# A new written-out order for a linear-attention and MLP kernel on one core, and shorter rows for the loads of r and v

## The chip, the cores and the metric

The kernel runs on one core of one Trainium2 chip. The metric is the device time of one execution in microseconds, the median of several runs. Engines are called as in the profile: PE is TensorE's matmuls and PEld its weight loads, DVE is VectorE, ACT is ScalarE, POOL is GpSimd, SP is SyncE. DMAs are issued by SP or by POOL.

## The reference

Four batches of eight heads run a recurrence over 768 steps with a state of 40x40 per head; its output, 3072 tokens of 320, goes through an MLP with softplus inside erf.

```
for t in range(768):
    y[:, :, t] = einsum('bhd,bhde->bhe', r_t, state)
    Sa = einsum('bhde,bhe->bhd', state, a_t)
    state = state * w_t[:, :, None, :] - einsum('bhd,bhe->bhde', Sa, b_t) \
          + einsum('bhd,bhe->bhde', v_t, k_t)
x = y.transpose(0, 2, 1, 3).reshape(3072, 320)
h = x @ w_in                      # 320 x 2048
out = (h * erf(softplus(h))) @ w_out   # 2048 x 320
```

## The kernel before

The recurrence is done in chunks of 32 steps. Two groups of 16 heads each run 24 chunks; four chunks (128 steps) make a stage, so there are 12 stages and 48 chunks. For each stage `prep` loads the decays w and makes their running products with two scans on VectorE (lines 631 and 635). For each chunk `aphase` loads k, b and a as one tile bk, scales it (lines 666 and 671), multiplies (A, line 676), masks (line 683), and sends a part to DRAM (AD). Once per stage `tphase` reads it back as Ti, solves a triangular system on VectorE by 28 short instructions (lines 723 and 724), sends the result out (TD) and back (Tb), transposes it (R, line 732) and finishes it with two groups of small matmuls (W and DAD, both line 739) and two VectorE steps (743, 746).

`chain` is what depends on the state, chunk after chunk: Z (line 784), a copy zt, U (line 793), a copy us into the tile Us, four transfers Vu<-Us, the transpose UT (line 820) of Us into pQ, the copy vtu into the tile vt, PQ (line 829) from vt, its mask on VectorE into Vu (line 832), MY (lines 840 and 844), and the update of the state MT (line 847) and of the output (Ym, line 851). vt is loaded for each chunk by one DMA called rv (line 770): r in two blocks of 32 columns, v in one, and the last 32 columns are filled by vtu. Every copy has line 570 on ScalarE or 572 elsewhere, every DMA line 575.

When a stage's outputs have gone through DRAM (xw, xr), the MLP takes its 256 tokens in eight tiles of 256 hidden columns: mm1 (line 1005, two blocks a tile), a copy hc, tanh, two logs, exp, two VectorE steps (1038, 1039), gelu, two more steps (1050, 1051), and mm2 (line 1060, four blocks a tile). Four tiles make a unit, which shares three loads of ScalarE's tables.

The MLP's weights come as 64-bit floats, and are taken apart at the start by VectorE, ScalarE and GpSimd (lines 931 to 962): from chunks of w_in in the tile wo, and of w_out in the tiles h.

All operations are first recorded by `Plan.add`, with what they read and write and which engines may do them. `Plan.schedule` could order them by its own rules, but when the tables ORDER and ENGINES fit, it takes them as they stand: ORDER is the order in which the operations are issued (each engine's instructions stand in its own queue in that order), ENGINES says who does each one, and an entry of −1 in ORDER is a filler, a matmul of constants into a bank that is not in use (`warm`, line 578). TensorE executes its queue in order, fillers too.

Of the kernel before, what the change touches and what calls it, by code (L numbers as in the profile page):

```python
# [1193 lines left out]
```

## Time and profile before

| what | value |
|---|---|
| median of 3 runs | 866.4 us (865.0 to 875.59) |
| the profiled execution, its own time | 870.61 us |
| its span, first to last instruction | 868.8 us |
| mean granted clock of TensorE | 0.959 |
| instructions | 32556, of them 13793 matmuls |
| DMA | 107.63 MB in 120213 packets |

Busy time is counted per engine; matmuls are pipelined, so a busy PE is not PE at its peak. "Idle before" is the time for which an engine stood still ahead of an instruction, with the last thing it waited for; "issue" is time in which nothing that the profile shows held it. The chain that ended last is followed back from the last instruction. A row of a timeline has its start, its length, the engine, the line and operation, out<-in, and in brackets the idle time before it.

### The profile page before, as it was taken

The numbers are of one execution on the slowest core, as the hardware profiler recorded it, in microseconds if no ns is written. First come the engines' busy times: TensorE is split into PE (matmuls) and PEld (weight loads), VectorE is DVE, ScalarE is ACT, GpSimd is POOL, SyncE is SP. The second block draws the span as 40 slices with busy tenths as digits, with TensorE's granted clock in tenths as the row PEclk, the third lists the DMA queues.
The fourth block names the chain that finished last, engine by engine and source line by source line (L and its number), as shares of the span: only waits on it lengthen the run. The fifth ranks groups of instructions, "written<-read, shape, count | busy, mean of one in ns | idle before, by whom it ended". The sixth has DMA issues, their size and how long they took to land.

```text
span 868.8 us, 32556 instructions
## 1 busy us (share of the span) xinstructions
PE 748.4 (86%) x13793; PEld 581.5 (67%) x13793; DVE 649.9 (75%) x1372; ACT 562.2 (65%) x1052; POOL 347.8 (40%) x493
## 2 busy tenths in 40 slices
...
PEclk9998999999999999998999899999998999998998
...
GB/s 238 200 182 171 181 155 147 116 144 125 143 118 138 144 151 107 133 135 113 159 119 122 119 141 130 145 99 165 119 144 101 102 117 96 71 62 53 19 15 19
DMA packets 120213, 107.63 MB, mean 124 GB/s; under 512 B 76397, under 2 KB 99285, under 8 KB 120061
## 3 DMA queue, kind: packets, MB, share of 16 engines
...
q8 instruction: 110, 1.80, 0.9%
...
## 4 chain that ended last, share of the span: by engine, by line
PE 40%; DMA 22%; DVE 16%; issue 10%; ACT 7%; POOL 3%; SPq 1%; DVEq 0%; POOLq 0%; ACTq 0%
PE po L1060 12%; PE ph L1005 10%; DMA Vu<-Us 5%; DMA Tb<-TD 3%; PE my L840 3%; DMA TD<-Ti 2%; DMA Zs<-Ab 2%; PE ph L578 2%; PE pA L739 2%; DMA AD<-Zs 2%; DVE nd L1038 2%; DVE h L1051 2%; PE pA L676 2%; PE pQ L811 2%; DMA Ti<-AD 2%
## 5 line engine op out<-in xcount | busy, mean ns | idle before, releaser
L1060 PE MATMUL po<-wo,h 128*128 128x320 f32 x768 | 254.6, 462 | 9.0 <-DVE h L1051 9.0
L1060 PEld LDWEIGHTS po<-wo,h 128*128 128x128 f32 x768 | 139.9, 199 | 54.3 <-DVE h L1051 10.1
L1013 ACT ACTIVATE l<-l 128x512 f32<-128x512 f32 x192 | 111.2, 625 | 15.8 <-DVE nd L1038 14.5
L1005 PE MATMUL ph<-xh,wih 128*128 128x256 f32 x384 | 99.9, 342 | 2.2 <-ACT h L570 1.2
L575 POOL DMA_DIRECT2D Vu<-Us x93 | 52.7, 570 | 113.7 <-ACT Us L570 73.4
L1005 PE MATMUL ph<-xl,wih 128*128 128x256 f32 x384 | 78.9, 287 | 2.1 <-issue 2.1
L1005 PE MATMUL ph<-xh,wil 128*128 128x256 f32 x384 | 78.2, 286 | 0.0
L840 PE MATMUL my<-Vu,sg 64*40 64x72 f32 x1536 | 53.5, 240 | 27.5 <-DMA Vu<-Us 16.6
L1051 DVE SCALAR_TENSOR_TENSOR h<-l,h 128x512 f32<-128x512 f32 x96 | 71.8, 757 | 5.1 <-POOL l L1050 4.3
L1039 DVE SCALAR_TENSOR_TENSOR r<-nd,r 128x512 f32<-128x512 f32 x96 | 70.7, 737 | 4.1 <-POOL nd L1038 3.0
L1005 PEld LDWEIGHTS ph<-xh,wih 128*128 128x128 f32 x384 | 63.8, 196 | 13.3 <-issue 1.9
L840 PEld LDWEIGHTS my<-Vu,sg 64*40 64x40 f32 x1536 | 40.9, 120 | 42.2 <-issue 11.9
L1013 ACT ACTIVATE l<-h 128x512 f32<-128x512 f32 x96 | 56.7, 627 | 12.0 <-DVE h L1051 8.3
L1038 DVE TENSOR_TENSOR nd<-l,r 128x512 f32<-128x512 f32 x79 | 55.1, 698 | 11.5 <-ACT r L1013 9.2
L578 PE MATMUL ph<-d 104*128 104x512 bf16 x256 | 63.6, 395 | 0.0
L1050 DVE TENSOR_TENSOR l<-l,r 128x512 f32<-128x512 f32 x77 | 58.3, 760 | 4.4 <-ACT l L1013 3.9
L1005 PEld LDWEIGHTS ph<-xl,wih 128*128 128x128 f32 x384 | 61.4, 196 | 0.0
L1005 PEld LDWEIGHTS ph<-xh,wil 128*128 128x128 f32 x384 | 60.9, 195 | 0.0
L570 ACT COPY Zm<-MT 40x320 f32<-40x320 f32 x63 | 28.7, 456 | 48.0 <-DVE MT L847 39.8
L570 ACT COPY h<-ph 128x512 f32<-128x512 f32 x79 | 45.7, 583 | 18.8 <-PE ph L1005 13.8
L676 PE MATMUL pA<-Ab,bk 104*64 104x64 f32 x720 | 32.6, 230 | 27.6 <-DVE bk L671 20.7
L1013 ACT ACTIVATE r<-r 128x512 f32<-128x512 f32 x96 | 55.2, 624 | 0.4
...
## 6 DMA issues: line engine op xcount, KB each, us to landing
bk<-in_kba_e POOLq DMA_DIRECT2D x26, 416.0 KB, 4.7
vt<-in_rv_e POOLq DMA_DIRECT2D x25, 416.0 KB, 4.5
vt<-in_rv_e SPq DMA_DIRECT2D x23, 416.0 KB
bk<-in_kba_e SPq DMA_DIRECT2D x19, 416.0 KB
...
```

Source lines behind the costliest of these rows:

```text
L570: self.nc.scalar.copy(o, i)
L575: self.P.add(name, "SP", lambda e: self.eng(e).dma_start(o(), i()), rd, wr, pr, ISSUE.get(name, 0.41))
L578: self.nc.tensor.matmul((self.ph[1], self.pQ)[x], self.d1[:, :128], self.d1[:, :512], start=True, stop=True)
L676: nc.tensor.matmul(pa[i % 2 * 64:i % 2 * 64 + 64, i // 4, i // 2 % 2], bk[:, i].rearrange("p a b -> p (a b)"), ab[:, :, i], start=True, st ...
L840: nc.tensor.matmul(my[h * 64:h * 64 + 40, x, j], sg[xs, j, h], vu[xs, j // 2 * 2 + h, j % 2], start=True, stop=False)
L1005: nc.tensor.matmul(ph[:, j * 256:j * 256 + 256], a[:k, fs], b[:k], start=(m == 0), stop=(m == 7))
L1013: self.P.add(name, "ACT", lambda e: nc.scalar.activation(out=o, in_=i, **kw), rd, wr + ["act"], pr, 0.62)
L1038: P.add("nd", [("DVE", 0.69), ("POOL", 1.28)], lambda e, r=r, l=l, nd=nd: s.eng(e).tensor_tensor(out=nd, in0=l, in1=r, op=ALU.mult), [("l" ...
L1039: P.add("rho", "DVE", lambda e, r=r, nd=nd: nc.vector.scalar_tensor_tensor(out=r, in0=nd, scalar=2 * C4, in1=r, op0=ALU.add, op1=ALU.mult) ...
L1050: P.add("E", [("POOL", 1.28), ("DVE", 0.69)], lambda e: s.eng(e).tensor_tensor(out=l, in0=l, in1=r, op=ALU.mult), [("r", ir)], [("l", il)] ...
L1051: P.add("G", "DVE", lambda e: nc.vector.scalar_tensor_tensor(out=h, in0=l, scalar=-1.0, in1=h, op0=ALU.add, op1=ALU.mult), [("l", il)], [( ...
L1060: nc.tensor.matmul(po, h[:, bs], s.wo[:, f], start=(f == 0), stop=(f == 15))
```

## The change

Four things change.

- ORDER and ENGINES are other tables of the same form. The count of fillers goes from 256 to 216. Of the operations that may be done by two engines, some change hands: VectorE has 1303 operations of the list (1332 before), ScalarE 1063 (1038), GpSimd 499 (489), SP 493 (500).
- rv has 80 rows instead of 104 and loads 96 of 128 columns. Before, the two heads of a pair began at rows 0 and 64 with 24 rows of zeros between; now they stand at 0 and 40, and the product over rows has 80 of them.
- Us is stored without gaps (four times 40 columns), is no longer zeroed at the start, and its transpose has 80 rows.
- A unit of the MLP is given as a list of sizes, [4] * 24, which gives the same units. The scratch size for DMA descriptors is written out with the value 16384, which is the default.

```diff
 ORDER = (
-    3, 7, 9, 20, 4, 6, 10, 18, 348, 144, 12, 22, 147, 11, 21, 145, 146, 16, 149, 23, 126, 129, 24, 148, 352, 135, 138, 351, 14, 17, 41, 53, 0, 15, 13,
+    7, 11, 143, 15, 16, 146, 19, 3, 6, 9, 8, 4, 17, 5, 144, 12, 22, 351, 23, 145, 21, 125, 128, 147, 148, 24, 126, 25, 0, 28, 134, 127, 152, 153, 27,
...
+SCRATCH = 16384
...
-    rv = np.zeros((NG, 24, 104, NP, 4, 32), np.float32)
-    rv[..., :2, :] = diag(el(r)).transpose(0, 1, 2, 4, 3, 5)
-    rv[..., 2, :] = stk(el(v))
-    o["rv_e"] = np.ascontiguousarray(rv[:, :, :, [pair(n) for n in range(NP)]]).reshape(NG, 24, 104, NP * 128)
+    rv = np.zeros((NG, 24, 2, 40, NP, 3, 32), np.float32)
+    for h in range(2):
+        rv[:, :, h, :, :, h] = el(r)[:, :, h]
+    rv[..., 2, :] = el(v)
+    o["rv_e"] = np.ascontiguousarray(rv[:, :, :, :, [pair(n) for n in range(NP)]]).reshape(NG, 24, 80, NP * 96)
...
-        s.US = ring("Us", K["us"], [128, NQ // 2, 128])
+        s.US = ring("Us", K["us"], [128, NQ, 40])
...
-        for n, R in (("zs", s.ZS), ("zm", s.ZM), ("us", s.US)):
+        for n, R in (("zs", s.ZS), ("zm", s.ZM)):
...
-        vr = s.VT[ivt]
+        vr = s.VT[ivt][:80]
...
-        s.dma("rv", lambda: vr, lambda: I["rv_e"][g, ck].rearrange("p (a x) -> p a x", a=NP), wr=[("vt", ivt, 0), ("vt", ivt, 1)], pr=prl)
+        s.dma("rv", lambda: vr[:, :, :96], lambda: I["rv_e"][g, ck].rearrange("p (a x) -> p a x", a=NP), wr=[("vt", ivt, 0), ("vt", ivt, 1)], pr=prl)
...
-                nc.tensor.transpose(put[:, y], us[:, y, 0:104], s.ident)
+                nc.tensor.transpose(put[:, y], us[:, 2 * y:2 * y + 2].rearrange("p h e -> p (h e)"), s.ident)
```

Line numbers after the change are one higher up to line 1020. Two places show what the tables move. First VectorE's queue in the solve of stage 0 (lines 723 and 724; 724 and 725 now), where an instruction that takes apart a chunk of w_out in the tile h (line 931, now 932) stands between the steps. Before:

```order
L723 TENSOR_TENSOR tmp_106<-Ti 128x50
L724 TENSOR_TENSOR Ti<-Ti,tmp_106 128x5x10
L931 TENSOR_SCALAR r_140<-h 128x512
L723 TENSOR_TENSOR tmp_106<-Ti 128x54
L724 TENSOR_TENSOR Ti<-Ti,tmp_106 128x6x9
```

Now:

```order
L724 TENSOR_TENSOR tmp_106<-Ti 128x56
L725 TENSOR_TENSOR Ti<-Ti,tmp_106 128x8x7
L932 TENSOR_SCALAR r_140<-h 128x512
L724 TENSOR_TENSOR tmp_106<-Ti 128x54
L725 TENSOR_TENSOR Ti<-Ti,tmp_106 128x9x6
```

It moved from behind the fifth step of the solve to behind the eighth. Second TensorE's queue at the first chunk of stage 3, around PQ (line 829, now 830) and the start of MY (lines 840 and 844, now 841 and 845); line 1060 is a block of mm2, lines 676 and 694 are the next stage's A and the transpose of its bk. Before:

```order
L1060 MATMUL po_161<-wo,h 128x320
L829 MATMUL pQ<-vt_107 64x2x32 x8
L676 MATMUL pA<-Ab_76,bk_100 64x2x32 x8
L840 MATMUL my<-Vu_78,sg_95 40x72 x4
L844 MATMUL my<-Rt_81,Sm_80 40x32 x4
```

Now:

```order
L677 MATMUL pA<-Ab_76,bk_100 64x2x32 x8
L830 MATMUL pQ<-vt_107 64x2x32 x8
L1060 MATMUL po_161<-wo,h 128x320
L695 MATMUL pA<-ident,bk_100 128x104 x4
L1060 MATMUL po_160<-wo,h 128x320
L841 MATMUL my<-Vu_78,sg_95 40x72 x4
L845 MATMUL my<-Rt_81,Sm_80 40x32 x4
```

The A block moved ahead of PQ, and two mm2 blocks and the transpose moved between PQ and MY.

More of the change, by code (lines that the diff above doesn't have):

```diff
@@ new lines @@
+    "AAAVGVVAAAVSAVVAVSVSSVPVVGGPAGGSGVPVVGSPVGGSGVPVVSSPAGVSSVPVVGSPAGGGGGVAPAPAAVAAPAPVPVPVVGSGGGAAPAPAAAAAPAPAPVPVVSSSGGAAPAPAAAAAPAPAPVPVVGGS"
+    "SSVAPAPAAVVAPVPAPVPVVSSSGGGGGAAVVVVVVVVVVVVVVVVVVVVVVVVVVVVGGGGVPPPPVPPPPVGAVGAVGGAGPPAAPPAAPPAAPPAAAAAAAAAAAAAAAAVVVVVVVVAAAAAPPVAPPAAVVPPP"
+    "PPPAAGVPPPPPPAAVVPPPPVVPPPPSAVVAVSVSGVPVVSGPASVGSVPVVSGPASVGSVPVVSGPAGVSSVPVVGSPASGGSSVVVPAPAGSSSPAPAPVPVVGGGGSAAPVPAGSSSPAPAPVPVVSGGGGVVPVP"
+    "ASSGGPVPAPVPVVGGGSGAAPAPAGGGSPAPAPVPVVSSGSGGGSAAVVVVVVVVVVVVVVVVVVVVVVVVVVVVSGSSVPPPPVPPPPVSAGSAGSGVVAAAAAAAAAAAAAAVVVVVVVVAAAAAPPVAPPAAGVPP"
@@ new lines @@
+    "PPPPAAGVPPPPPPAAVVPPPPVVPPPPASASAAAAAAAAAAAAAAVVGVVVVVAAAAAPPAAPPAAVVPPPPPPAAGVPPPPPPAAVVPPPPVVPPPPSAVVVVGGGGGPVVSGPVSGSGVPVVSGPVGGGGVPVVGGP"
+    "AGVSSVPVVSSPAGGSGGGAAPAPASGSSPVPVPVPVVSSSSSAAPAPASGSGPAPAPVPVVSSSGSAVPAPAGGGGPAPAPVPVVGSGGSAAPAPVGGSGPAPAPVPVVGSGSSGGSAAVVVVVVVVVVVVVVVVVVVV"
+    "VVVVVVVVGSSGVPPPPVPPPPVGVVSAVGSVVAAAAAAAAAAAAAAVVVVGVVVAAAAAPPAAPPAAVVPPPPPPAAVVPPPPPPAAVVPPPPVVPPPPASASAAAAAAAAAAAAAAVVVVGVGVAAAAAPPAAPPAAV"
+    "VPPPPPPAAVVPPPPPPVAGVPPPPVVPPPPSAVVVVGVSGVPVVGSPAGVSSVPVVGSPVGVSSGPVVSGPAGVGGGPVVGSPAGGSSSVAAPVPAGSGSPAPAPVPVVSSGSSAVPVPASGGSPVPAPVPVVSSGSGA"
@@ new lines @@
+    "APAPAGGSSPAPAPVPVVSSGGGAAPAPAGGSGPAPAPVPVVSSSGSGGSAAVVVVVVVVVVVVVVVVVVVVVVVVVVVVSSGSVPPPPVPPPPVSVGSAGSSVGAAAAAAAAAAAAAAGVGVVVVVAAAAAPPAAPPAA"
+    "VVPPPPPPAAVVPPPPPPAAVVPPPPGVPPPPASASAAAAAAAAAAAAAAVVVVVVVVAAAAAPPAAPPAAVVPPPPPPAAVVPPPPPPAAGVPPPPVVPPPPGAVVAVSGSSVPVVSGPVSGGSVPVVSGPAGVSSGPV"
+    "VSGPAGVGGVPVVSSPAGSGSSVVAPAPASGSGPAPAPVPVVSGSSSVAPVPVGGSSPVPVPVPVVSSSSSAAPAPASGSSPAPAPVPVVSGSGSAVPAPASSGGPAPVPVPVVSGSSGGGGAAVVVVVVVVVVVVVVVV"
+    "VVVVVVVVVVVVGSGSVPPPPVPPPPVGVGGVGSGVVAAAAAAAAAAAAAAVVVVGVVVAAAAAPPAAPPAAVVPPPPPPVAGVPPPPPPAAVVPPPPGVPPPPASASAAAAAAAAAAAAAAVVVVVVVVAAAAAPPAAP"
@@ new lines @@
+    "PAAVVPPPPPPAAVVPPPPPPAAVVPPPPGVPPPPGAVVAVSVSSVPVVGSPVGVSSVPVVSGPAGVSGVPVVGGPAGVGSVPVVGSPVGGSSGVAAPAPASGSSPAPVPVPVVSGGSSVVPAPVGSSSPAPAPVPVVSG"
+    "SSGAVPAPASSSSPAPAPVPVVSGGSGAAPAPAGGSGPAPAPVPVVGSSSGGSGAAVVVVVVVVVVVVVVVVVVVVVVVVVVVVSGGGVPPPPVPPPPVSAGGVVGGAVAAAAAAAAAAAAAAVVGVGVVVAAAAAPPAA"
+    "PPAAVVPPPPPPAAVVPPPPPPAAVVPPPPVVPPPPASASAAAAAAAAAAAAAAVVVVVVVVAAAAAPPVAPPAAVVPPPPPPAAGVPPPPPPAAVVPPPPVVPPPPGAVVAVSVSGVPVVGGPVGVSSVPVVSSPAGVG"
+    "SVPVVSSPAGVGSVPVVSSPAGSGGGVAAPVPAGGSSPAPVPVPVVGGSSSVVPAPVGSSSPAPAPVPVVSGSSGAAPAPAGSGGPAPAPVPVVSSGSSAAPAPASSSSPAPAPVPVVGSSSGGGSAAVVVVVVVVVVVV"
@@ new lines @@
+    "VVVVVVVVVVVVVVVVGGGGVPPPPVPPPPVSAGGAVSSAVAAAAAAAAAAAAAAVVVVVVVVAAAAAPPAAPPAAVVPPPPPPAAVVPPPPPPAAVVPPPPVVPPPPASASAAAAAAAAAAAAAAGVVVVVGVAAAAAP"
+    "PAAPPAAGVPPPPPPAAVVPPPPPPAAVVPPPPGVPPPPGAVVAVGVGGGPVVGSPAGVSSVPVVSGPAGVSSVPVVSGPVSVGSVPVVSSPASSGSGVVVPVPAGGSSPAPAPVPVVGGSGGAAPVPVSGSGPAPVPVP"
+    "VVSGSSSVAPVPVGSSGPAPAPVPVVSGSSSAAPAPAGSSSPAPAPVPVVSGSGGGGSAAVVVVVVVVVVVVVVVVVVVVVVVVVVVVGGGGVPPPPVPPPPVGAGGAVGSAGAAAAAAAAAAAAAAGVVVVVVVAAAAA"
+    "PPAAPPAAVVPPPPPPAAVVPPPPPPAAVVPPPPVVPPPPASASAAAAAAAAAAAAAAVVVVVVVVAAAAAPPAAPPAAVVPPPPPPAAGVPPPPPPAAVVPPPPGVPPPPGAVVAVGVSSVPVVSGPAGVGSVPVVGSP"
@@ new lines @@
+    "AGVSSVPVVGSPASVGSGPVVSSPASSGSGVAAPAPVSSGSPAPAPVPVVSSSSSVVPVPVGGGSPVPVPVPVVSSSSGAAPAPAGGGGPAPAPVPVVGGSSSAAPAPAGGGSPAPAPVPVVSGSSGGSSAAVVVVVVVV"
+    "VVVVVVVVVVVVVVVVVVVVSSSSVPPPPVPPPPVSAGSVVGSAVAAAAAAAAAAAAAAVVVVVVVVAAAAAPPAAPPAAVVPPPPPPAAVVPPPPPPAAGVPPPPVVPPPPASASAAAAAAAAAAAAAAGVGVVVVVAA"
+    "AAAPPAAPPVAVVPPPPPPAAVVPPPPPPAAGVPPPPVVPPPPSAVVAVSVGSVPVVSSPAGGGSVPVVSSPAGVGSGPVVSSPAGVGGVPVVGGPAGSSGGVAVPAPASSGSPAPAPVPVVSGSGGVAPAPASSGSPVP"
+    "APVPVVSSGSSAAPAPASGGGPAPAPVPVVGSSGGAAPAPAGGGSPAPAPVPVVGSSSSSSGAAVVVVVVVVVVVVVVVVVVVVVVVVVVVVGSGGVPPPPVPPPPVGVGGAGSGAGAAAAAAAAAAAAAAGVVVVVVVA"
@@ new lines @@
+    "AAAAPPAAPPAAVVPPPPPPAAVVPPPPPPVAVVPPPPVVPPPPASAGAAAAAAAAAAAAAAVVVVVVVVAAAAAPPVAPPAAVVPPPPPPAAGVPPPPPPAAVVPPPPVVPPPPSAVVAVSVSSVPVVSGPASGGSGPV"
+    "VSGPAGVGSVPVVSGPVGVSSVPVVGSPASSSSGVVAPVPAGSGGPVPVPVPVVSSGSGAAPAPAGGGSPVPVPVPVVGSSGGAAPAPVSGGSPAPAPVPVVSGSSSAVPAPAGSGSPAPAPVPVVSSGGGSSSAAVVVV"
+    "VVVVVVVVVVVVVVVVVVVVVVVVGGGGVPPPPVPPPPVSVGSVGSSAGAAAAAAAAAAAAAAVVVVVVVVAAAAAPPAAPPVAVVPPPPPPAAVVPPPPPPVAVVPPPPGVPPPPASASAAAAAAAAAAAAAAGVVVVV"
+    "VVAAAAAPPVAPPAAVVPPPPPPAAVVPPPPPPVAVVPPPPVVPPPPGGGGSVAAPAPVGGSSPAPVPVPVVGSSGSVVPAPAGGSSPVPAPVPVVGSSSGVAPAPVSSSGPAPVPVPVVGSGSSVVPVPVGGGSPAPAP"
@@ L234 @@
+    "VPVVGSSSVPVVSVGSVGSSVVAAAAAAAAAAAAAAVVVVVVVVAAAAAPPAAPPAAVVPPPPPPVAVVPPPPPPAAVVPPPPVVPPPPVSVSAAAAAAAAAAAAAAVVVVVVVVAAAAAPPVAPPAAVVPPPPPPAAVV"
+    "PPPPPPAAGVPPPPGVPPPPAAAAAAAAAAAAAAVVVVVVVVAAAAAVVPPPPVVPPPPVVPPPPVVPPPPASAS"
 )
+SCRATCH = 16384
 PARAMS = dict(K=dict(warm=43.6))
@@ L814, in chain @@
         P.add("ysM", [("ACT", 0.43), ("DVE", 0.48)], lambda e: s.copy(e, sm, restride(pt[:, :, 0:80].rearrange("p a (h e) -> p a h e", h=2), 2, 64)), ["pQ", "pQb"], [("sm", ism)], pr)
-        put = s.pQ[0:104, 256:512].rearrange("p (y f) -> p y f", f=128)
+        put = s.pQ[0:80, 256:512].rearrange("p (y f) -> p y f", f=128)
         def mmut(e):
             for y in range(NQ // 2):
-                nc.tensor.transpose(put[:, y], us[:, y, 0:104], s.ident)
+                nc.tensor.transpose(put[:, y], us[:, 2 * y:2 * y + 2].rearrange("p h e -> p (h e)"), s.ident)
         P.add("UT", "PE", mmut, [("us", iu, "-"), "ident"], ["pQb"], pr, 0.25)
-        P.add("vtu", [("ACT", 0.37), ("DVE", 0.42)], lambda e: s.copy(e, vr[:, :, 96:], put.rearrange("p y (z s) -> p (y z) s", s=32)), ["pQb"], [("vt", ivt, 1)], pr)
+        P.add("vtu", [("ACT", 0.37), ("DVE", 0.42)], lambda e: s.copy(e, vr[:, :, 96:], s.pQ[0:80, 256:512].rearrange("p (a s) -> p a s", s=32)), ["pQb"], [("vt", ivt, 1)], pr)
         pq = s.pQ[:, :256].rearrange("p (y h l t) -> p y l h t", y=2, h=2, t=32)
@@ L1018, in tanh, with unit @@
         s.act("tanh", n, s.LL[il], s.H[ih], [("h", ih)], [("l", il)], pr, func=AF.Tanh, scale=0.5)
-    def unit(self, u, pr):
+    def unit(self, ns, pr):
         s, nc, P = self, self.nc, self.P
-        ns = range(s.K["un"] * u, s.K["un"] * u + s.K["un"])
         sl = lambda n: (n % len(s.H), n % len(s.LL), n % len(s.RR), n % len(s.ND))
@@ L1088, in tph @@
             N.tphase(q // NS, q % NS, t(q, 0) - amargin + 15)
-        UN, nb = N.K["un"], 8 * nst
+        sizes, nb = N.K["units"], 8 * nst
+        first = [sum(sizes[:i]) for i in range(len(sizes) + 1)]
+        assert first[-1] == nb
         at_ = dict(mm1=0, unit=0)
@@ L1096, in mlp @@
                 at_.update(mm1=0, unit=0)
-            N.load_x(q, m(8 * q / UN) - 10)
+            N.load_x(q, m(2 * q) - 10)
             def mm1(n):
                 while at_["mm1"] <= n:
-                    N.mm1(at_["mm1"], m(at_["mm1"] // UN) - D)
+                    N.mm1(at_["mm1"], m(max(x for x in first if x <= at_["mm1"]) / 4) - D)
                     at_["mm1"] += 1
```

65 lines of the change are left out of this document (19 added, 46 removed), and 359 rows, old and new, of the table ORDER.

## The prediction

> **What bounds the kernel now.** I read the page first (busy shares, the chain that ended last), then the busy time by stretch, then the chain inside the start-up, then the waits of TensorE, and last the DMA issues.
>
> ```profile
> span 868.8 us, 32556 instructions
> PE 748.4 (86%) x13793; PEld 581.5 (67%) x13793; DVE 649.9 (75%) x1372; ACT 562.2 (65%) x1052; POOL 347.8 (40%) x493
> PEclk9998999999999999998999899999998999998998
> PE 40%; DMA 22%; DVE 16%; issue 10%; ACT 7%; POOL 3%; SPq 1%; DVEq 0%; POOLq 0%; ACTq 0%
> ```
>
> TensorE is busy 86% of the span, yet only 40% of the last chain is TensorE's: the rest is latency (DMA 22%, VectorE 16%). So the kernel is near TensorE's bound and loses time to waits in TensorE's in-order queue. Where, the table of busy time by stretch tells (us of stretch, then busy us of PE, PEld, DVE, ACT, POOL, the granted clock, DMA share, GB/s):
>
> ```profile
> 0.00:40.00 40.00, 12.70 (x122) 8.55 (x123) 31.43 (x49) 20.05 (x38) 18.45 (x29) 1.00 0.83 234
> 40.00:69.60 29.60, 23.74 (x112) 10.71 (x111) 24.72 (x58) 15.11 (x30) 7.94 (x13) 0.96 0.63 167
> 69.60:118.00 48.40, 46.94 (x1015) 27.18 (x1016) 37.70 (x91) 23.05 (x54) 17.05 (x24) 0.95 0.60 163
> 118.00:142.00 24.00, 19.53 (x585) 14.50 (x583) 16.60 (x31) 9.04 (x20) 18.02 (x23) 1.00 0.63 168
> 142.00:807.00 665.00, 596.84 (x11723) 483.45 (x11723) 502.93 (x1091) 452.52 (x846) 283.22 (x406) 0.96 0.48 121
> 807.00:868.80 61.80, 48.69 (x242) 37.16 (x240) 36.54 (x56) 42.45 (x68) 3.10 (x2) 0.95 0.04 12
> ```
>
> Three parts: a start-up of 142 us before the MLP runs in earnest, a middle of 665 us in which TensorE idles 68 us, and a tail of 62 us. The tail holds nearly the same work in both orders. In the start-up TensorE looks full (46.94 of 48.40 us), but much of that is the fillers of line 578, matmuls without use:
>
> ```profile
> L578 PE MATMUL ph<-d 104*128 104x512 bf16 x256 | 63.6, 395 | 0.0
> 40.48 23.26 PE L578 MATMUL ph<-d 104*128 104x512 bf16 x107
> by line: PE ph L578 23.1%; issue 9.8%; DMA Zs<-Ab 8.0%; DMA xd<-Pr 5.2%; PE pA L676 4.7%; PE pA L739 3.9%; DMA xr<-xd 3.8%; PE my L840 3.4%; PE pA L694 3.2%; PE pQ L829 3.1%; PE ph L1005 2.7%; DVE r L932 2.4%; DVE bk L671 2.4%; ACT l L934 2
> 71.60 3.76 PE ph L578 x11
> 91.34 1.62 PE ph L578 x7
> 95.54 2.70 PE ph L578 x12
> ```
>
> The second row gives one filler's price in a run: 23.26/107 = 0.217 us. The third is the chain between 64 and 145 us: 23.1% of these 81 us, 18.7 us, are fillers. Real matmuls stood behind them with their operands ready: the fillers do not fill waits there, they make some.
>
> **The change part by part.** *Fillers.* ORDER holds 256 entries of −1 before and 216 now. By the two lists, 117 stand ahead of the first W (line 739) before and 106 now, and behind it 139 and 110. The 11 ahead of W buy nothing, since W waits for something else (next item). The 29 behind W lie on the chain in part: 139 of them make 18.7 us of it, 0.135 us each, so 29 × 0.135 = 3.9 us; if each counts in full, 29 × 0.217 = 6.3 us. What is late next are VectorE and the copies between the steps of stage 0; if they held the same times without the fillers, the gain would be 0. I take −5 us, bounds −6.3 and 0.
>
> *The way to the first W.* W needs the transposed Tb, and that comes at the end of the solve on VectorE:
>
> ```profile
> 54.39 0.43 DVE L931 TENSOR_SCALAR r<-h 128x512 int32<-128x512 int32 x1 [3.71 <-DMA h<-in_moe_w_out]
> 68.87 0.70 DVE L732 STREAM_TRANSPOSE T<-Tb 128x512 f32<-128x512 f32 x1
> 69.67 0.55 PE L739 MATMUL pA<-T,Ap 32*32 32x32 f32 x25 [5.94 <-issue]
> ```
>
> A weight instruction waited 3.71 us for its load with the solve queued behind it. The first pair of lists above, in the section on the change, shows the place. The waiting instruction moved three solve steps later, so that the 3.71 us shrink, at best to nothing. Against it, VectorE has more ahead of the transpose: two more L936 and two more L671 (0.68 us a row, as below), one more L931 (0.43, above), two memsets and a copy, less one copy (some 0.5 together), in all about 3.7 us.
>
> ```profile
> 70.48 0.68 DVE L936 TENSOR_TENSOR wo<-l,r 128x512 f32<-128x512 f32 x1
> 72.02 0.68 DVE L671 TENSOR_TENSOR bk<-bk,Wt 104x512 f32<-104x512 f32 x1
> ```
>
> Net 0, bounds −3.7 and +3.7.
>
> *The middle.* The MLP blocks are spread over the 48 chunks as before (when chunk 47's MY ends, 171 mm1 and 320 mm2 blocks are done before, 174 and 318 now). What moved is the spacing inside a chunk. The second pair of lists above shows one chunk of stage 3. Between PQ and MY VectorE must mask pQ (L832). In that chunk one block of TensorE stood there, three do now. Over the last 40 chunks a single block stood there 28 times, now 13 times; on average 1.5 blocks before, 2.3 now; from U to MY 6.9 and 7.4. In exchange U to UT, which covers the copy of Us, falls from 3.6 to 2.9. The waits that this touches, TensorE's and its weight load's between 142 and 807 us, and that copy:
>
> ```profile
> PE my L840 <- DMA Vu<-Us: 16.6, 12, 2.2
> PEld my L840 <- DVE Vu L832: 9.7, 16, 1.9
> L570 ACT COPY Us<-my 128x160 f32<-128x160 f32 x33 | 9.6, 291 | 27.6 <-PE my L793 20.0 <-DVE r L1039 6.3 <-DMA Rt<-in_r_e 1.0
> ```
>
> If the mask's wait goes in the 15 chunks that gained blocks, 15 × 9.7/16 = 9 us go; half a block more from U to MY (a block is 254.6/384 = 0.66 us by L1060, quoted below) takes 12 × 0.3 = 4 us from the wait for Vu. At worst the copy shows in each of 40 chunks: 40 × 0.29 = +12 us; at best both waits vanish: −26 us. I take −5: about half of the 13, because less cover for UT gives part of it back.
>
> ```profile
> L1060 PE MATMUL po<-wo,h 128*128 128x320 f32 x768 | 254.6, 462 | 9.0 <-DVE h L1051 9.0
> ```
>
> *Issuers.* By the table of engines VectorE has 29 operations fewer, mostly copies that went to ScalarE and eleven xl that went to GpSimd, about 9 us of 650; ScalarE has about 9 us more of 562. Both have room beside TensorE in the middle (502.93 and 452.52 of 665), so I cost this at 0; if ScalarE became the bound in the stretch of a stage, its 9 us would show.
>
> *The rows of r and v.* 48 loads shrink from 104 rows of 4096 bytes to 80 rows in 8 pieces of 384 bytes: 8.7 MB of 107.63 less, but 640 pieces instead of 104.
>
> ```profile
> L575 POOL DMA_DIRECT2D vt<-in_rv_e x25: 552/578/613, 66.5 to 770.7; - x25
> L575 SPq DMA_DIRECT2D vt<-in_rv_e x23: 318/380/1392, 14.7 to 780.9; - x23
> L575 POOL DMA_DIRECT2D Tb<-TD x14: 822/838/862, 64.3 to 538.9; - x14
> L575 SPq DMA_DIRECT2D Tb<-TD x10: 612/635/749, 292.9 to 734.9; - x10
> vt<-in_rv_e POOLq DMA_DIRECT2D x25, 416.0 KB, 4.5
> Tb<-TD POOLq DMA_DIRECT2D x14, 128.0 KB, 3.3
> ```
>
> Tb is loaded in 1024 pieces of 128 bytes; taking its price for the 640, an issue costs 0.26 us more on either queue, 48 × 0.26 = 12 us spread over two queues. The loads are issued a chunk ahead and no wait of TensorE ends on them, so 0; where such an issue stands ahead of a Vu<-Us of the same queue it costs 0.26 us, in 24 chunks 6 us. Landing stays between 3.3 and 4.5 us. The memset of Us and 24 columns of the transposed Us go, worth nothing on the path.
>
> The Trainium skill, page "DMA: Bandwidth & Descriptors", section "Specifications", speaks against this edit: below 512 bytes a piece the engines read, modify and write. By it 240 KB would cost like 480, thus land later than the 416 KB now; by the row of Tb, 128-byte pieces land in 3.3 us, and I see no such cliff. Either way the sum stays, as the load is covered.
>
> *Sum.* The profiled execution took 870.6 us (span 868.8 and 1.8 around it), 4.2 above the median of 866.4. 870.6 − 5 + 0 − 5 + 0 = 860.6, less 4.2: **856 us**.
>
> **The rivals.** *Nothing measurable* (866 us): the start-up is bound by the weights on VectorE, and the waits at MY only move to UT. For it: VectorE is busy 31.43 of the first 40 us and 37.70 of the 48.40 behind the first W. Against it: 18.7 us of fillers on the chain.
>
> *The waits really go* (843 us): both MY waits vanish (−26 instead of −5) on top of the −5 of fillers, less some 8 us given back at other steps: 866.4 − 23. For it: MY is waited for by everything in a chunk. Against it: Us is copied with less cover.
>
> *The solve falls behind on GpSimd's queue* (879 us). Of the solve's transfers Ti goes from 12 on POOL to 17 and Tb from 14 to 17, while xl goes there eleven times more.
>
> ```profile
> L1050 POOL TENSOR_TENSOR l<-l,r 128x512 f32<-128x512 f32 x19 | 26.9, 1416 | 31.6 <-DVE l L1050 15.8 <-ACT l L1013 14.9 <-DVE r L1039 0.8
> L989 POOL TENSOR_TENSOR xl<-xr,xh 128x256 fp32r<-128x256 f32 x7 | 5.5, 784 | 5.5 <-ACT xh L570 5.5
> POOL Tb L575 <- DMA TD<-Ti: 31.2, 7, 19.4
> ```
>
> If each of the 8 stands behind one such pair, 8 × (1.42 + 0.78) = 17.6 us; with the fillers' −5 that is 866.4 + 12.6. It decides once Tb lands after TensorE has run out of blocks between its last A and W. Against it: in most stages the list of TensorE holds blocks worth some 30 us there, nearly as many as before.
>
> *The clock closes* (872 us). The clock already fell to 0.95 in the stretch with TensorE's gap of 5.94 us. With 29 fillers fewer more gaps appear; real matmuls there are 46.94 + 19.53 − 30 = 36 us (139 × 0.217 = 30), and a third of them at half clock costs 12 us, less 6 of fillers. The Trainium skill, page "TensorE: Matmul & The Clock Gate", section "Part 1: The HAM clock gate", says that an idle window of about 3.4 us halves the clock; the row of 5.94 us agrees, and no other gap of that length stands in this stretch.
>
> **How the numbers follow.** Forecast 0.44, nothing measurable 0.24, waits go 0.14, solve behind 0.09, clock 0.09. 2% is about what a measurement of this kernel can tell from no change: below 849 or above 884. Faster by more: the 0.14 and the low edge of the forecast, 0.16. Slower by more: half of the solve rival and a little, 0.06. Within: 0.78. The range reaches from 840 (three us beyond the waits that go) to 876 (four beyond the clock), which leaves out the solve rival and the far ends of the bounds.
>
> **What would show it.** Right: L578 down to 216 and about 10 us less busy, its share of the chain in the start-up down; first mm1 5 us sooner; the waits of L840's new line for L832's and for Vu<-Us smaller; vt loads at some 0.64 us on SP. Wrong: the first W later than 73 us, a granted clock below 0.93 before 142 us, or a longer time between the first mm1 and 807 us than 665.

## The result, and the profile after

The changed kernel takes 825.69 us (median of 4 runs, 821.56 to 829.33); the kernel before, run beside it, takes 869.22. The ratio is 0.9492, with a 95% interval of 0.9411 to 0.9573: 5.1% faster, below the predicted range. The profiled execution took 821.56 us, 49 less than the one of before. That pair makes the gain look larger than it is: 821.56 is the fastest of four executions, 870.61 lies above the median of before, and the medians are 43.5 us apart.

Page of the changed kernel: span, busy shares, granted clock, the chain that ended last, DMA traffic.

```profile
span 819.8 us, 32461 instructions
PE 728.6 (89%) x13753; PEld 567.6 (69%) x13753; DVE 635.4 (78%) x1343; ACT 568.8 (69%) x1077; POOL 352.8 (43%) x503
PEclk9999897999999999999999999999999999999997
PE 48%; DMA 15%; DVE 13%; ACT 10%; issue 8%; POOL 3%; SPq 2%; DVEq 0%; POOLq 0%; ACTq 0%
DMA packets 128728, 98.98 MB, mean 121 GB/s; under 512 B 88112, under 2 KB 111264, under 8 KB 128576
```

Against before: TensorE is busy 19.8 us less (728.6, not 748.4), with only 40 matmuls fewer, and 48% of the chain is its work instead of 40%, while DMA fell from 22% to 15%. The clock row has a single 7 and a single 8 ahead of its last slice. Busy time by stretch, with the borders put at places much like those of before (us of stretch, busy us of PE, PEld, DVE, ACT, POOL, granted clock, DMA share, GB/s):

```profile
0.00:40.00 40.00, 14.22 (x128) 9.25 (x129) 31.99 (x57) 21.38 (x40) 14.79 (x27) 1.00 0.82 228
40.00:63.80 23.80, 20.63 (x96) 9.14 (x94) 21.31 (x57) 11.64 (x24) 6.00 (x9) 1.00 0.78 210
63.80:114.70 50.90, 44.03 (x927) 24.89 (x927) 32.37 (x79) 23.19 (x57) 18.84 (x25) 0.90 0.55 128
114.70:137.00 22.30, 16.87 (x476) 12.08 (x476) 15.18 (x30) 8.32 (x20) 15.03 (x20) 0.77 0.65 170
137.00:759.00 622.00, 583.64 (x11894) 475.14 (x11893) 499.67 (x1069) 461.63 (x871) 293.89 (x421) 0.99 0.48 118
759.00:819.80 60.80, 49.20 (x239) 37.10 (x237) 34.88 (x56) 42.60 (x69) 4.22 (x4) 0.93 0.04 14
```

The start-up gives 5 of the 49 us (142 to 137), the tail 1, the middle 43 (665 to 622). These borders are near one another, but are not the same event. From the end of MY in chunk 7 to its end in chunk 47, an exact pair, the time falls by 43 as well, from 620.0 to 577.0 us. In the middle TensorE idles 622 − 583.64 = 38.4 us instead of 68.2, which is 29.8 of the 43; the other 13.2 are busy time, with some 170 matmul records more than before, not fewer. The same work took less time because the granted clock was 0.99 instead of 0.96. One stretch from each kernel, the stage from chunk 27 to 31, one of the two stages that differ most, shows the pair, first before, then after:

```profile
474.00:543.00 69.00, 60.71 (x1150) 48.48 (x1149) 51.70 (x112) 46.69 (x87) 27.72 (x40) 0.95 0.52 131
```

```profile
461.00:518.00 57.00, 54.05 (x1117) 43.67 (x1116) 48.21 (x109) 44.00 (x84) 25.94 (x40) 1.00 0.51 131
```

A mean of 0.96 hides how the clock is lost. In both traces it is granted either in full or in half, and half in pieces of 3.4 us or of two such lengths in the middle. There are 13 such places in the middle before, 58 us in all, and 4 after, 13.7 us. Each of the 17 begins right behind 3.4 us in which TensorE was busy for 61% or less, with one wait of 1.3 us or more in or at the end of it; at 8 of the 13 and at 3 of the 4 the longest such wait is MY's. One place of before, with MY's wait and the two lengths of 3.41 us on either side of the fall (TensorE busy 1.64 of 3.41 us, then the clock at 0.50):

```profile
564.56 0.37 PE L840 MATMUL my<-Vu,sg 64*40 64x72 f32 x5 [1.77 <-DMA Vu<-Us]
562.27:565.68 3.41, 1.64 (x81) 1.42 (x77) 3.08 (x4) 2.45 (x5) 1.32 (x2) 1.00 0.40 123
565.68:569.09 3.41, 3.41 (x26) 2.45 (x15) 2.82 (x6) 3.22 (x6) 0.86 (x2) 0.50 0.00 0
```

The wait for MY in the middle, as a group of TensorE's instructions (busy us and mean ns, then the idle time ahead of them and what ended it). Before:

```profile
L840 PE MATMUL my<-Vu,sg 64*40 64x72 f32 x1376 | 48.7, 241 | 27.0 <-DMA Vu<-Us 16.6 <-DVE Vu L832 3.3 <-issue 3.2
```

And after, with the two rows of the weight load's waits that answer to the 9.7 us for the mask before, and to 9.0 for Vu:

```profile
L841 PE MATMUL my<-Vu,sg 64*40 64x72 f32 x1408 | 45.6, 232 | 14.2 <-DMA Vu<-Us 5.2 <-DMA vt<-in_rv_e 2.8 <-DVE Vu L833 2.6
...
PEld my L841 <- DVE Vu L833: 5.4, 9, 2.0
PEld my L841 <- DMA Vu<-Us: 4.1, 5, 2.1
```

MY accounts for 12.8 us of the 29.8 that TensorE no longer idles. The other 17 are spread over many smaller waits of other lines. Last the start-up, the fillers and the loads of r and v (groups, timeline, issues with min/median/max ns, landing in us):

```profile
L579 PE MATMUL ph<-d 104*128 104x512 bf16 x216 | 57.5, 416 | 0.0
...
35.44 25.19 PE L579 MATMUL ph<-d 104*128 104x512 bf16 x106
63.87 1.93 PE L740 MATMUL pA<-T,Ap 32*32 32x32 f32 x128 [3.24 <-issue]
...
L576 POOL DMA_DIRECT2D vt<-in_rv_e x24: 727/738/797, 27.1 to 712.2; - x24
L576 SPq DMA_DIRECT2D vt<-in_rv_e x24: 585/610/1488, 91.4 to 726.2; - x24
vt<-in_rv_e POOLq DMA_DIRECT2D x24, 240.0 KB, 4.0
```

The first W starts at 63.87 instead of 69.67 us, with a gap of 3.24 us ahead of it instead of 5.94. The lead doesn't last: the first mm1 starts at 135.3 us, 3 later than before (132.3).

### The profile page after: what moved, and what is told of

Its sections match the earlier page's. It is cut to its first block, busy times and chain, and to the rows that moved or that the text cites. A ratio compares the mean times of both kernels' runs of the same rounds, so it can differ in the third digit from the quotient of the medians.

```text
span 819.8 us, 32461 instructions
## 1 busy us (share of the span) xinstructions
PE 728.6 (89%) x13753; PEld 567.6 (69%) x13753; DVE 635.4 (78%) x1343; ACT 568.8 (69%) x1077; POOL 352.8 (43%) x503
## 4 chain that ended last, share of the span: by engine, by line
PE 48%; DMA 15%; DVE 13%; ACT 10%; issue 8%; POOL 3%; SPq 2%; DVEq 0%; POOLq 0%; ACTq 0%
PE po L1060 17%; PE ph L1006 12%; DMA Vu<-Us 3%; PE pA L740 3%; PE my L841 3%; ACT r L1014 3%; ACT l L1014 2%; PE pA L677 2%; DMA Tb<-TD 2%; PE my L785 2%; PE my L794 2%; SPq L576 2%; DMA wo<-in_moe_w_in 2%; PE pQ L812 2%; PE pQ L830 2%
## 5 line engine op out<-in xcount | busy, mean ns | idle before, releaser
L1060 PE MATMUL po<-wo,h 128*128 128x320 f32 x768 | 250.7, 455 | 6.1 <-DVE h L1051 5.3
L1060 PEld LDWEIGHTS po<-wo,h 128*128 128x128 f32 x768 | 136.7, 195 | 49.0 <-DVE h L1051 7.0
L576 POOL DMA_DIRECT2D Vu<-Us x88 | 49.5, 567 | 115.1 <-ACT Us L571 76.1
L1006 PE MATMUL ph<-xh,wih 128*128 128x256 f32 x384 | 97.5, 335 | 0.8 <-ACT h L571 0.8
L1039 DVE SCALAR_TENSOR_TENSOR r<-nd,r 128x512 f32<-128x512 f32 x96 | 67.9, 707 | 4.6 <-POOL nd L1038 2.8
L841 PE MATMUL my<-Vu,sg 64*40 64x72 f32 x1536 | 49.4, 232 | 14.3 <-DMA Vu<-Us 5.2
L579 PE MATMUL ph<-d 104*128 104x512 bf16 x216 | 57.5, 416 | 0.0
L841 PEld LDWEIGHTS my<-Vu,sg 64*40 64x40 f32 x1536 | 37.3, 115 | 28.3 <-issue 6.0
L1050 DVE TENSOR_TENSOR l<-l,r 128x512 f32<-128x512 f32 x75 | 52.1, 701 | 3.2 <-ACT l L1014 2.6
L1014 ACT ACTIVATE r<-l 128x512 f32<-128x512 f32 x96 | 54.5, 619 | 0.0
```

What stands on the lines that cost most here:

```text
L576: self.P.add(name, "SP", lambda e: self.eng(e).dma_start(o(), i()), rd, wr, pr, ISSUE.get(name, 0.41))
L579: self.nc.tensor.matmul((self.ph[1], self.pQ)[x], self.d1[:, :128], self.d1[:, :512], start=True, stop=True)
L841: nc.tensor.matmul(my[h * 64:h * 64 + 40, x, j], sg[xs, j, h], vu[xs, j // 2 * 2 + h, j % 2], start=True, stop=False)
L1006: nc.tensor.matmul(ph[:, j * 256:j * 256 + 256], a[:k, fs], b[:k], start=(m == 0), stop=(m == 7))
L1014: self.P.add(name, "ACT", lambda e: nc.scalar.activation(out=o, in_=i, **kw), rd, wr + ["act"], pr, 0.62)
L1039: P.add("rho", "DVE", lambda e, r=r, nd=nd: nc.vector.scalar_tensor_tensor(out=r, in0=nd, scalar=2 * C4, in1=r, op0=ALU.add, op1=ALU.mult) ...
```

## Experiments

All ratios are to the kernel before on the same chip, with a 95% interval; the changed kernel is 0.949. Chips differ by about 1%, so ratios are compared, not times.

**Rows or order.** First the change was cut in two: the short rows of r and v and the compact Us with the tables of before, and the new tables with the rows and Us of before.

```diff
# rows only: the changed kernel's code
-ORDER, ENGINES = (new tables)
+ORDER, ENGINES = (tables of before)
# order only: the changed kernel's tables
-        vr = s.VT[ivt][:80]
+        vr = s.VT[ivt]
-        s.US = ring("Us", K["us"], [128, NQ, 40])
+        s.US = ring("Us", K["us"], [128, NQ // 2, 128])
```

> The order and the issuers of before with the short rows of r and v (and Us without gaps). The gain to explain is 5.1%. Theory O (the order of the table makes it): no change, 869 us within 8. Theory R (8.7 MB less and shorter loads let the chain's transfers Vu<-Us land sooner): at least a third of the gain, under 855 us, with TensorE's wait for Vu<-Us well under 16.6 us.

> The order and the issuers of after with the long rows of before (Us is zeroed once by GpSimd beside another memset). Theory O: 826 us within 8. Theory R: the part of the rows is missing, over 840 us.

Rows only: 0.9754 [0.9667, 0.9841]. Order only: 0.9629 [0.9525, 0.9733]. Both parts count, about 2.5 and 3.7 points, and together they give 5.1. The prediction had the rows at nothing.

What each part removes is not the same. From the end of MY in chunk 7 to its end in chunk 47, in this order: before, rows only, order only, both (columns as in the tables by stretch):

```profile
178.10:798.10 620.00, 559.03 (x11158) 450.28 (x11154) 469.41 (x1009) 420.81 (x787) 267.81 (x381) 0.96 0.48 121
178.10:778.40 600.30, 544.48 (x11154) 441.09 (x11154) 468.39 (x1009) 421.38 (x787) 271.46 (x381) 0.98 0.47 114
182.30:778.80 596.50, 551.65 (x11174) 446.36 (x11174) 463.19 (x988) 427.94 (x808) 269.82 (x386) 0.98 0.50 126
174.00:751.00 577.00, 543.76 (x11174) 441.10 (x11174) 461.66 (x988) 427.24 (x808) 272.18 (x386) 0.99 0.48 118
```

The rows alone take 19.7 us off, 14.6 of them busy time and 5.2 idle time; the order alone 23.5, of them 16.1 idle and 7.4 busy; both together 43.0. With the rows in place, the order takes 22.6 us of idle time and 0.7 of busy time. So the rows act mostly through the clock, the order mostly through the waits. These are single executions, but the mean clock of all executions on that chip agrees: 0.968 to 0.974 in four executions with the rows only, 0.950 to 0.968 in five with the order only, 0.954 to 0.969 in seven of the kernel before.

**Order and issuers apart.** Each table was joined with the other one of before.

```diff
# new order, old issuers
-ENGINES = (new table)
+ENGINES = (table of before)
# old order, new issuers
-ORDER = (new table)
+ORDER = (table of before)
```

> The order of after, but each operation on the engine that did it before; short rows. If the order alone makes the gain (theory O), 830 us within 8. Theory I (order and issuers were found together, and the order needs its own issuers): half of the gain or more is lost, over 848 us.

> The order of before with the issuers of after; short rows. Theory O: 869 us within 10. Theory I in its strong form (it is the move from VectorE to ScalarE and of DMAs to the other queue): under 850 us.

1.1548 [1.1449, 1.1647] and 1.1473 [1.1381, 1.1564]: 15% slower either way. From the page of each, the busy share and the clock:

```profile
PE 792.5 (79%) x13753; PEld 607.5 (61%) x13753; DVE 653.7 (65%) x1372; ACT 561.8 (56%) x1051; POOL 351.6 (35%) x493
PEclk9998977867889888999989898898989979999998
```

```profile
PE 792.8 (80%) x13793; PEld 612.6 (61%) x13793; DVE 645.5 (65%) x1343; ACT 570.8 (57%) x1077; POOL 350.9 (35%) x503
PEclk9989886889988998988899899787999797899998
```

Apart from the 40 fillers, the engines have no more instructions than in the kernel that the table of issuers comes from. TensorE's busy time is 44 us higher than before at a mean clock of 0.90, and it waits longer: 60.9 and 52.7 us of idle time ahead of MY in the whole kernel, 27.5 before. A reason that fits, though no run isolates it: an operation given to another engine takes the place in that queue which the order gives it, and what it waits for then holds that engine's next work too. So the price of the issuers can't be read from the work that each engine gains or loses, and the two tables can't be priced apart.

**What about the rows.** The new code with rows of 4096 bytes in one piece, 104 of them as before, or 80.

```diff
-        s.dma("rv", lambda: vr[:, :, :96], lambda: I["rv_e"][g, ck]...)
+        s.dma("rv", lambda: s.VT[ivt], lambda: I["rv_e"][g, ck]...)    # 104 rows
+        s.dma("rv", lambda: vr, lambda: I["rv_e"][g, ck]...)           # 80 rows
```

> After, with the compact Us and the product over 80 rows kept, but rv loaded as before the change: 104 rows of 4096 bytes (rows 80 to 103 and the last 32 columns are padding that nothing uses or that is overwritten). Theory T (the rows' gain is the transfer's time on the DMA engines, which other transfers stand behind): the gain of the rows is lost, 840 us within 6, and AD<-Zs lands at about 3.0 us again instead of 2.3. Theory G (the gain is in the shorter geometry on TensorE and the compact Us): no change, 826 us.

> After, with rv loaded as 80 rows of 4096 bytes (the last 32 columns are zeros that are overwritten): 320 KB in 80 pieces, between the 416 KB in 104 and the 240 KB in 640. If the bytes and engines decide (theory T), it lies between, 830 to 835 us; if the small pieces cost on the DMA engines, it is as fast as after or faster, 826 us or less, with a cheaper issue on SP (0.38 instead of 0.61 us).

104 rows: 0.9669 [0.9605, 0.9734]; 80 rows: 0.9477 [0.9389, 0.9565]. The long load alone costs what the whole old form costs, so the compact Us and the products over 80 rows are worth nothing that shows, and the load is all of it. That 240 KB in pieces of 384 bytes and 320 KB in pieces of 4096 give the same time could mean that the pieces cost nothing, or that they cost what the fewer bytes save. The traces speak for the second: a packet of 384 bytes took 27.7 ns on average (the loads that SP issues), one of 4096 bytes 241 ns in the run with 80 long rows (all packets of that size), so a load is 640 × 27.7 = 17.7 us of DMA engine time against 80 × 241 = 19.3. Per byte the small pieces cost about 1.2 times as much. Two more sizes were to tell the number of bytes from the number of rows that each DMA engine gets.

```diff
-        s.dma("rv", lambda: vr[:, :, :96], lambda: I["rv_e"][g, ck]...)
+        s.dma("rv", lambda: s.VT[ivt][:96], lambda: I["rv_e"][g, ck]...)
+        s.dma("rv", lambda: s.VT[ivt][:88], lambda: I["rv_e"][g, ck]...)
```

> The changed kernel with each load of r and v as 96 rows of 4096 bytes, 384 KB in one piece of DRAM (80 such rows gave 0.948, 104 gave 0.967). Theory of bytes: what counts is how much a load moves; by a straight line from 320 to 416 KB 0.960, and more than for 88 rows. Theory of rows per engine (rows are dealt out in equal shares, so 80 rows make 5 for each of 16 engines, 96 make 6 for each of 16, 88 make 8 for each of 11, 104 make 8 for each of 13): 0.954 or less, and less than for 88 rows.

> As the run with 96 rows, but 88 rows of 4096 bytes, 352 KB. Theory of bytes: 0.954, below the run with 96 rows. Theory of rows per engine: 0.965 or more, above the run with 96 rows and close to that with 104.

96 rows: 0.9628 [0.9564, 0.9692]; 88 rows: 0.9603 [0.9547, 0.9659]. In order of bytes: 240 KB 0.949, 320 0.948, 352 0.960, 384 0.963, 416 0.967. Against the rows per engine speaks that 96 rows lie above the 0.954 that it allowed, and 88 no higher than 96. The order by bytes holds, though neighbours can't be told apart and the step from 320 to 352 is larger than a straight line gives. In the middle, with the same order throughout, the traces show the loss in both forms (us from MY's end in chunk 7 to its end in chunk 47, one execution each, on different chips):

| KB a load | time | TensorE idle | at half clock |
|---|---|---|---|
| 416 | 599.6 | 42.8 | 44.4 |
| 384 | 588.3 | 38.6 | 23.9 |
| 352 | 588.2 | 38.1 | 23.9 |
| 320 | 583.6 | 35.6 | 20.5 |
| 240 | 577.1 | 33.3 | 13.7 |

Waits of TensorE over 2 us number 7 in the first row, 5 in the second and 3 in the others. Which transfer comes later beside a longer load is not settled. The load's own landing doesn't tell: with 80 long rows it lands in 4.4 us, with 104 in 4.4 too.

```profile
vt<-in_rv_e POOLq DMA_DIRECT2D x24, 320.0 KB, 4.4
Zs<-Ab POOLq DMA_DIRECT2D x36, 40.0 KB, 4.2
```

```profile
vt<-in_rv_e POOLq DMA_DIRECT2D x24, 416.0 KB, 4.4
Zs<-Ab POOLq DMA_DIRECT2D x36, 40.0 KB, 3.8
```

I had taken it that other transfers land sooner beside a shorter load, since Zs<-Ab fell from 3.9 to 2.7 us in the changed kernel; in the run with 80 long rows it is back at 4.2 and the time is as good. That reason falls.

**Start or middle.** The tables were joined at MY of chunk 7.

```diff
# old start, new middle
+ORDER, ENGINES = before's up to MY of chunk 7, the new ones for what is left
# new start, old middle: the other way round
```

> Short rows; order and issuers of before up to the MY of chunk 7 (the first two stages, with all 256 fillers), those of after from there on. If the order's gain lies in the middle (theory M): 830 us, 4 to 6 above after. If it lies in the start-up (theory S, my prediction's fillers): 845 us or more.

> Short rows; order and issuers of after up to the MY of chunk 7, those of before from there on. Theory M: 847 us, a few below the 851 of the old order with short rows. Theory S: 835 us or less.

0.9438 [0.9354, 0.9522] with the old start, 0.96 [0.9531, 0.9669] with the old middle. The 29 fillers behind W and the earlier first W are not needed for the gain. Ahead of the old middle the new start is worth about 1.5 points (0.975 to 0.960, the intervals just touching); ahead of the new middle it is worth nothing. The two gains don't add.

**The spacing at MY.** If the gain of the middle is that MY finds its mask and Vu done, moving blocks must do it in both orders. In the old order 28 blocks of mm1 and mm2 were moved from behind MY to ahead of it, in the new order 46 the other way. A piece of TensorE's queue in the new order:

```diff
 UT
 A
 PQ
 mm2
-mm2
 MY
+mm2
```

> The order and the issuers of before with the short rows (the kernel that measured 0.975), but 28 blocks of mm1 and mm2 are moved ahead of MY, so that in chunks 8 to 47 at least two blocks of TensorE stand between PQ and MY (1.5 on average there before, 2.2 now). Theory of spacing (the gain of the new middle is that MY no longer waits for the mask and for Vu, and that TensorE, with fewer gaps, keeps its clock): at least one point better than 0.975, so a ratio of 0.965 or less, with a smaller wait of TensorE for Vu<-Us and a higher granted clock in the middle. Rival (the gain comes from the whole timing of the order and its issuers, not from this spacing): 0.970 to 0.985, whatever the waits at MY do.

> The changed kernel, but 46 blocks of mm1 and mm2 that stand between PQ and MY are moved right behind MY, so that 36 of 40 chunks have at most one block there (2.3 on average before, 1.15 now). Theory of spacing: at least 1.5 points worse than 0.949, so 0.965 or more, with the wait for the mask and for Vu back to the size of the kernel before. Rival (whole timing): 0.943 to 0.957.

Old order spaced: 0.9773 [0.9723, 0.9824], no gain over 0.9754. New order unspaced: 0.9657 [0.9578, 0.9736], 1.65 points lost. My theory held on one side and fell on the other, so two things were open: whether any 46 moves hurt, and why the old order gains nothing. The first was tried with 46 other moves, all between one MY and the next PQ, and with 13 blocks more ahead of MY.

```diff
# other moves
-mm2
 bT
+mm2
# more spacing, where fewer than two blocks stood between PQ and MY
+mm2
 MY
-mm2
```

> The changed kernel with 46 blocks of mm1 and mm2 moved by one step of the chunk, as many as in the run without spacing, but all of them between one MY and the next PQ: the blocks between PQ and MY stay at 2.3 on average. Theory of spacing: the ratio stays at that of the changed kernel, 0.943 to 0.957. Rival (any hand-made move spoils an order that was found as a whole): as the run without spacing, 0.960 or more.

> The changed kernel with 13 blocks moved ahead of MY, so that no chunk from 8 to 47 has fewer than two blocks between PQ and MY (2.6 on average, 2.3 before the moves). Theory of spacing: 13 waits for the mask or Vu of some 0.4 to 1 us go, so 0.935 to 0.945. Rival (the order is at its floor, or moves hurt): 0.947 or more.

Other moves: 0.9534 [0.9472, 0.9597], as the changed kernel. More spacing: 0.9525 [0.946, 0.959], no further gain. Then 65 blocks behind MY:

> The changed kernel with 65 blocks moved behind MY: 0.7 blocks stand between PQ and MY on average in chunks 8 to 47 and none in 19 chunks (2.3 in the changed kernel; 1.15 gave 0.966). Theory of spacing: the loss grows as the cover shrinks, by 0.7/1.15 x 1.6 = at least half a point to one point more: 0.970 or more, with TensorE's idle time at MY in the middle above the 14.2 us of the changed kernel by 12 us or more. Rival (the 1.6 points came from something else in those moves): 0.960 to 0.968.

0.9801 [0.9761, 0.9841]. With 2.6, 2.3, 1.15 and 0.7 blocks on average the ratios are 0.953, 0.949, 0.966 and 0.980: above two blocks no change is clear of the noise, below it the loss grows. The busy row of the middle of the last one, and its MY:

```profile
137.00:800.00 663.00, 598.88 (x11932) 492.03 (x11929) 498.32 (x1071) 461.81 (x870) 294.92 (x422) 0.97 0.46 112
L816 PE MATMUL my<-Vu,sg 64*40 64x72 f32 x1408 | 50.7, 240 | 36.4 <-DMA Vu<-Us 13.4 <-DVE Vu L808 13.1 <-DMA vt<-in_rv_e 3.5
```

Against the changed kernel TensorE idles 36.4 − 14.2 = 22.2 us more at MY, 3.5 more elsewhere (27.7 and 24.2), and is busy 598.9 − 583.6 = 15.3 us more at a clock of 0.97 instead of 0.99. The stretch is 41 us longer, but this pair overstates the loss: by the ratios it is 3.1 points, some 27 us, and the two executions come from different chips. The run of the section "Pieces put together" (the new middle with 2.6 blocks, 80 long rows) ran on the same chip. From MY of chunk 7 to MY of chunk 47, first 0.7 blocks, then 2.6:

```profile
178.00:792.10 614.10, 554.95 (x11172) 453.82 (x11172) 458.76 (x988) 427.98 (x809) 272.57 (x386) 0.97 0.45 111
175.30:761.10 585.80, 551.59 (x11178) 445.19 (x11176) 459.52 (x987) 426.43 (x805) 273.20 (x386) 0.98 0.47 116
```

Here 28.3 us of time go with 24.9 us of idle time, all of it at MY (34.7 and 9.5 us), and 3.4 of busy time. So a us of idle time cost a little over one, and 1.6 in the other pair (41 us for 25.7), where the times at half clock lie further apart (41.0 and 13.7 us there, 41.0 and 27.3 here). That removed cover costs time is shown by moving blocks alone.

Why the old order gains nothing from spacing, its rows tell in part. Rows only, then the same with spacing (busy by stretch, then MY):

```profile
142.00:788.00 646.00, 583.81 (x11811) 474.82 (x11810) 502.74 (x1093) 454.61 (x849) 289.25 (x409) 0.98 0.47 113
L817 PE MATMUL my<-Vu,sg 64*40 64x72 f32 x1376 | 45.6, 231 | 22.3 <-DMA Vu<-Us 12.1 <-DVE Vu L809 4.3 <-DVE xh L549 1.7
```

```profile
142.00:792.00 650.00, 590.40 (x11751) 474.42 (x11737) 505.95 (x1090) 453.89 (x848) 288.67 (x407) 0.97 0.46 113
L817 PE MATMUL my<-Vu,sg 64*40 64x72 f32 x1376 | 45.2, 233 | 16.4 <-DMA Vu<-Us 10.2 <-DVE Vu L809 3.1 <-DVE Zs L660 1.5
```

The wait at MY does shrink by 5.9 us. But 3.3 of them come back as idle time elsewhere (40 to 43 us: the blocks are missing where they were taken), the wait for Vu stays the larger part, and TensorE's busy time is 6.6 us more (two executions on two chips). The new order idles only 24 us outside MY. So the spacing at MY is needed for the gain and is not all of it; no single edit was found for the other 16 us.

**A later mask.** Without moving anything, the mask was written twice in each chunk (the second writes the same again), in the changed kernel and in the kernel with the rows only.

```diff
+            for _ in range(2):
                 nc.vector.tensor_tensor(out=vu[:, :, :, 40:72]..., in0=s.pQ[:, :256]..., in1=s.tri..., op=ALU.mult)
```

> The changed kernel with the mask of pQ written twice in each chunk (the second operation writes the same again): MY becomes ready 0.42 us later in 48 chunks, and VectorE is 20 us busier. Theory of spacing: the new order has blocks in front of MY, so it pays only where the mask already ended a wait: 11 x 0.42 = 5 us, up to 8, a ratio of 0.954 to 0.960, and less than the old order pays. Rival (VectorE or the clock pay whatever the spacing): as much as the old order, 10 us or more.

> The order and issuers of before with the short rows (0.975) and the mask of pQ written twice. Theory of spacing: the mask ended a wait in 26 chunks of that kernel, so 26 x 0.42 = 11 us or more, a ratio of 0.987 or more. Rival: as much as the new order pays with its second mask.

0.9512 [0.9436, 0.9588] and 0.9809 [0.9741, 0.9877], so 0.2 and 0.55 points above their baselines. MY's idle time rose as follows, first in the new order (14.2 before), then in the old (22.3 before):

```profile
L821 PE MATMUL my<-Vu,sg 64*40 64x72 f32 x1408 | 44.5, 230 | 16.5 <-DVE Vu L811 7.5 <-DMA Vu<-Us 4.3 <-DMA vt<-in_rv_e 2.6
```

```profile
L822 PE MATMUL my<-Vu,sg 64*40 64x72 f32 x1376 | 46.9, 234 | 26.8 <-DVE Vu L812 13.4 <-DMA Vu<-Us 8.9 <-DVE xh L549 1.7
```

The direction is as the spacing has it: of 48 × 0.42 = 20 us of later masks the new order pays 2.3 and the old one 4.5 at MY. But both are below what I had expected, and the intervals overlap, so these two runs show the idle time and not the time. They also show that 18 us more on VectorE in the middle of the new order (517.8 of 623 us busy) cost less than can be told, within about a point.

**Pieces put together.** The old start, the new middle with more spacing, and 80 long rows.

> The order and issuers of before up to MY of chunk 7, from there the new order with at least two blocks between PQ and MY, and the loads of r and v as 80 rows of 4096 bytes: three edits that each were no worse than the changed kernel. If their gains add up (0.5 point for the start, 0.2 for the rows): 0.940 or less, below the interval of the changed kernel. If they were only scatter: 0.943 to 0.957.

0.9491 [0.9448, 0.9534]: scatter. No version here beats the changed kernel.

## Why the prediction was wrong, step by step

*What bounds the kernel* was right: TensorE near its bound, the loss in waits of its queue. The faults are in the size of the removed waits and in the loads put at nothing.

*Fillers and the way to the first W* (−5, and 0 within 3.7). The fillers went as listed (216, 106 of them ahead of W), for 6 us less busy time instead of 10. The first W came 5.8 us sooner, more than the bound of 3.7. But the first mm1, forecast 5 us sooner, came 3 us later, and the run with the old start is as fast as the changed kernel: ahead of the new middle this term gave nothing that shows. The clock rival was right in the place: between 114.7 and 137 us the clock fell to 0.77 (1.00 before), and with it the sign that was named for being wrong, a clock below 0.93 before 142 us, came true. That stretch idles 5.4 of its 22.3 us; before it idled 4.5 of 24.0 at a clock of 1.00, so the sum of the idle time alone doesn't tell when the clock falls. What tells is how much of it falls into one length of 3.4 us; it need not be all of that length, as the clock rival had it: counted in the lengths of 3.41 us between which the clock changes, it fell in the middle of both traces behind each one that was busy for half or less.

*The middle* (−5, bounds −26 and +12) is one of the two terms that failed, by its size: the stretch lost 43 us, of which some 20 came with the rows of r and v and some 23 with the order. The mechanism, waits at MY that shrink as blocks move ahead of it, is borne out by the run with 0.7 blocks. I priced the waits at MY from 26 us and took a fifth of them. On TensorE's own row they fell by 12.8 us, near the 13 that I had worked out before I halved it; 4.7 of these came with the rows alone (27.0 to 22.3) and 8.1 with the order (22.3 to 14.2). What I lacked is that I looked at one place of each chunk: with the rows in place the order took 23.8 us of idle time off (62.2 to 38.4), so nearly 16 went at other lines, which a count of blocks at MY can't see. The clock I used only as a risk: of 51 us at half clock between MY of chunk 7 and MY of chunk 47 the rows alone leave 20.5, the order alone 27.3, both 13.7. My fear that less cover for UT would give part of it back did not come true: TensorE's idle time ahead of that line in the middle was 3.9 us before and is 0.4 now.

*Issuers* (0) can't be judged as a term: the runs with one table exchanged are 15% slower. What I worked out, the engine's busy time, was right in kind (VectorE 14.5 us less, ScalarE 6.6 more, some 9 expected of each) and beside the point.

*The rows of r and v* (0) is the second failure, and here the mechanism was wrong: they measured 2.5 points, some 20 us. The price of the issue was about right (610 and 738 ns, 0.64 and 0.84 expected), and so was the landing (4.0 us). Wrong was the conclusion "no wait of TensorE ends on them, so 0". The load's length costs time in waits that don't name it, and above all in the clock behind them: with the rows alone the busy time of the same matmuls fell by 14.6 us and TensorE's idle time by 5.2. That the load holds up other transfers on the DMA engines fits this, but which ones stays open. The rule of the Trainium skill, page "DMA: Bandwidth & Descriptors", section "Specifications", by which pieces under 512 bytes are read, modified and written, would by the estimate of the prediction make 240 KB cost like 480; the times show no sign of it (0.949 with such pieces, 0.948 with 320 KB in long ones). Nor do the packets, with 1.2 times the engine time per byte.

*The tail* was right: 60.8 us for 61.8.

*The rivals.* "The waits really go" (843, 0.14) came nearest, but for part of the reason: the two rows of MY's waits that it took fell from 26.3 to 10.6 us and did not vanish, and the other lines, the rows of r and v and the clock are not in it. "Behind on GpSimd's queue" did not happen: Tb<-TD lands in 3.5 us (3.3 before), and the first W came sooner. The range was too narrow because its lower end took only the waits at MY, nothing for the rows, and none of the 68 us of idle time and 4% of clock that stood in the quoted row.
